# Moving sixteen partition-half swaps from VectorE to GpSimd in a convolution + MLP kernel, with a new instruction order

## The chip, the cores and the metric

The kernel runs on one core of one Trainium2 chip. The metric is the device time of one execution in microseconds (us). Several executions are timed and their median is used; a further execution is recorded by the hardware profiler, and all durations below come from that one.

## The reference

Two layers are applied one after the other to x, 2048 rows by 512 columns in bf16. Each layer is a gated long convolution (A) followed by an MLP (B), each behind a layernorm and with a residual. The convolution's k, v and filters are the same in both layers, so its result y is computed once.

```
kv = (sum over 4 taps of k shifted down by 0..3 rows, times shift_k) * v
y  = irfft(rfft(kv, 4096) * rfft(ssm_k, 4096))[:2048] + kv * ssm_D
twice:
    x = x + layernorm(x) * y
    z = layernorm(layernorm(x))
    x = x + gelu(z @ w1 + b1) @ w2 + b2      # w1 512 x 1376, w2 1376 x 512
```

## The kernel before

**Convolution.** The 2048 rows are split in two halves of 1024, and a Fourier transform of each half is done as matmuls. `stage1` (matmul L630) multiplies the data with a cosine/sine table, `stage2` (matmul L644) with the 4 MB table `tab_s`, which is loaded in four pieces of 1 MB; each of its eight groups needs one half of one piece. A spectrum lies with its real parts in one half of the partitions and its imaginary parts in the other. A complex product therefore needs the filter's spectrum twice: once as it is, and once with the two halves exchanged. The exchange is `swap_v` (L663 on): one 64-partition copy for each half. For the first half of the rows the filter's spectrum is in C3 and the exchanged copy goes to C4, in four pieces, each after two groups of `stage2`; for the second half it goes from C6 to C4. That makes 8 + 8 = 16 copies, all on VectorE (L669). The products follow (`tt`, L534), then the inverse transform: `inverse1` (L682) and `inverse2` (L697). `turn_h` and `turn_k` transpose inputs (L571, L589), and `taps` does the first half's shifts as matmuls (L609) that VectorE multiplies with v (L614). Every matmul group ends with an eviction from PSUM to SBUF by ScalarE (L544) or VectorE (L545).

**MLP.** Eight blocks of 512 rows. For each: statistics (`bn_stats` L894, aggregate L896, a small scaling L901), the power -0.5 on GpSimd (L902), a small VectorE step (L904), normalisation on either engine (L941 ScalarE, L942 VectorE), a transposition by a DMA on SyncE's queue (L999; by TensorE, L1007, for the first block), eleven column groups of the first matmul (L1022) with gelu on ScalarE (L1027), and the second matmul (L1042) with the residual added on VectorE (L1046). The four blocks of the first 1024 rows run while the second half's convolution is spread between their matmuls; then come the four others.

**Order.** Each operation is recorded with an engine (or two to choose from), a duration in ns and what it reads and writes. `schedule` then places them one after the other on each engine by priority, and `sync` adds semaphore waits. The table of numbers handed to `schedule` shifts the priority of single operations. The result is a fixed order for each engine, which runs its list strictly in that order. On GpSimd each instruction that is not the first also waits for the one before it:

```
if e == POOL and o.pos and known[e].get(e, -1) < o.pos - 1:
    need[e] = q[o.pos - 1]
```

The first use of the power L902 makes the compiler put a GpSimd library reload directly ahead of it (MODIFY_POOL_CONFIG in the trace). Before the change, GpSimd has nothing to do but eight small fills, this reload and the 24 powers.

A GpSimd form of the copy is there already, switched off by the flag `PSW` (for the first half alone); it addresses the same bytes as 32-bit words through `W32`:

```
if pool:
    i2, o2 = W32(64 * h, 64, src0 + dg0 * 128 + k0, nd, nk), W32(64 - 64 * h, 64, dst0 + dg0 * 128 + k0, nd, nk)
    P.op(POOL, lambda e, i2=i2, o2=o2: e.tensor_copy(o2, i2), 1500.0, reads=[i], writes=[o])
```

Of the kernel before, what the change touches and what calls it, by code (L numbers as in the profile page):

```python
# [12 lines left out]
PE, ACT, DVE, POOL, SP = "tensor", "scalar", "vector", "gpsimd", "sync"  # L13
# [405 lines left out]
                getattr(block, e)(body)  # L419


WF, SPL, NA1, NDX, KP, KM, SG, PG, PSW, PLN, END, SPS, ST4, IA, SWA = 8, 1, 0, 64, 2, 0, 1, 1, 0, 0, 1, (0, 4), 0, 0, 0
S, D, FF = 2048, 512, 1376
B = 1024
EPS = 1e-5
# [36 lines left out]
AR = 105728  # L462


def bass_interleave_layers__ssm_conv_h3__mixer_channel_mlp__prompt_kernel(
        nc, A_q, A_k, A_v, A_shift_k, A_ssm_k, A_ssm_D, B_x, B_w1, B_b1, B_w2, B_b2, out):
    P = Prog(nc)
# [5 lines left out]
    def A(p0, n, off, *dims):  # L473
        return bass.AP(ar, p0 * AR + off, [[AR, n]] + [list(d) for d in dims])
# [7 lines left out]
    def QB(tile, p0, n, off, *dims):  # L482
        whole = bass.AP(ps, 0, [[4096, 128], [1, 4096]]).bitcast(BF16)
        return bass.AP(whole.tensor, p0 * 8192 + tile.base * 1024 + off, [[8192, n]] + [list(d) for d in dims])
# [6 lines left out]
    def place(n):  # L491
        o = pos[0]
        pos[0] += n
        return o
# [5 lines left out]
    C1, C3, C4, C5, C6 = (place(8192) for _ in range(5))  # L500
# [38 lines left out]
    def evac(dst, src, tile, engs=None, dur=EVD):  # L539
        engs = engs or EV[0]  # L540

        def f(e):
            if e is nc.scalar:
                return e.activation(dst, src(), AF.Copy)  # L544
            return e.tensor_copy(dst, src())  # L545
        return P.op(engs, f, dur, writes=[dst], tile=tile, early=True)
# [109 lines left out]
    def W32(p0, n, off, nd, nk):  # L656

        whole = bass.AP(ar, 0, [[AR, 128], [1, AR]]).bitcast(mybir.dt.int32)
        return bass.AP(whole.tensor, (p0 * AR + off) // 2, [[AR // 2, n], [64, nd], [1, nk // 2]])

    def swap_v(dst0, src0, k0, nk, dg0=0, nd=64, pool=0):
        for h in range(2):
            i = A(64 * h, 64, src0 + dg0 * 128 + k0, [128, nd], [1, nk])  # L663
            o = A(64 - 64 * h, 64, dst0 + dg0 * 128 + k0, [128, nd], [1, nk])
            if pool:
                i2, o2 = W32(64 * h, 64, src0 + dg0 * 128 + k0, nd, nk), W32(64 - 64 * h, 64, dst0 + dg0 * 128 + k0, nd, nk)
                P.op(POOL, lambda e, i2=i2, o2=o2: e.tensor_copy(o2, i2), 1500.0, reads=[i], writes=[o])
            else:
                P.op(DVE, lambda e, i=i, o=o: e.tensor_copy(o, i), 710.0, reads=[i], writes=[o])  # L669

# [70 lines left out]
    for i in range(KP):  # L741
        n = 4096 // KP
# [23 lines left out]
    for i in range(WF):  # L766
        tl = Tile(fill, 0, 8)
        P.op(PE, lambda e, tl=tl, w=w, m=m: e.matmul(Q(tl, 0, 128, 0, [1, 512]), w, m, start=True, stop=True), 216.0,
             reads=[w, m], tile=tl, ni=2, prio=-1e7 - i)
# [10 lines left out]
    for b in range(4):  # L780
        o, i = A(0, 128, R_DG + b * 512, [128, 4], [1, 128]), A(0, 128, R_ID, [0, 4], [1, 128])
        P.op(DVE, lambda e, tl=tl, o=o, i=i, b=b: e.tensor_tensor(o, i, QB(tl, 0, 128, b, [4, 4], [0, 128]), ALU.mult), 620.0,
             reads=[i], writes=[o], tile=tl)
    for i in range(2):
        d0 = A(0, 128, HR[0] + i * 2048, [1024, 2])
        P.op(DVE, lambda e, d0=d0, tl=tl, i=i: e.tensor_tensor(d0, d0, QB(tl, 0, 128, 16 + 2 * i, [1, 2]), ALU.add), 150.0,
             reads=[d0], writes=[d0], tile=tl)
    for j2 in range(2):
# [4 lines left out]
        def f(e, ins=ins, tl=tl):  # L793
            for o, w, m in ins:
                r = e.matmul(Q(tl, 0, 128, o, [1, 128]), w, m, start=True, stop=True)
            return r
# [10 lines left out]
    for g in range(8):  # L807
        stage2(C1, C3, 0, g)
        if g % 2:
            swap_v(C4, C3, 32 * (g // 2), 32, pool=PSW)  # L810
# [33 lines left out]
    for w in range(2 if SG else 4):  # L844
        (shift if SG else shift1)(w)
        n = 4 if SG else 2
        stage1([(KV[1], 0)], C1, 1, range(n * w, n * w + n))
    load_q(1)
    for g in range(4):
        swap_v(C4, C6, 0, 128, 16 * g, 16)  # L850
    for g in range(0, 8192, 4096 if PG else 2048):
        for p in (C6, C4):
            n = 4096 if PG else 2048
            o = A(0, 128, p + g, [1, n])
# [24 lines left out]
    for i in range(2):  # L879
        o = A(96, 1, R_HT + 6144 + i * 512, [1, 512])  # L880
# [55 lines left out]
    def norm(s, mr, o):  # L936
        x = A(0, 128, XS[s], [1, 512])

        def f(e):
            if e is nc.scalar:  # L940
                return e.activation(o, x, AF.Identity, bias=mr[2], scale=mr[1])  # L941
            return e.tensor_scalar(o, x, mr[0], mr[1], ALU.subtract, ALU.mult)  # L942
        if len(mr) == 2:
            P.op(DVE, f, 350.0, reads=[x] + mr, writes=[o])
        else:
            P.op((ACT, DVE), f, {ACT: 715.0, DVE: 340.0}, reads=[x] + mr, writes=[o])
# [3 lines left out]
    def ntmp():  # L950
        nn[0] += 1
        return R_N + (nn[0] % 6) * 512
# [9 lines left out]
    BYPE = (0,)  # L962
    for L, b in [(0, 0), (0, 1), (1, 0), (1, 1), (0, 2), (0, 3), (1, 2), (1, 3)]:
        lo = 2 if b < 2 else 0
        k = blk[0]
# [8 lines left out]
        def lean(i):  # L974
            P.boost = {e: bo[e] + (3e5 if k in SPS and i < 2 else 0.0) for e in bo}
# [17 lines left out]
        for i, s in enumerate(sl):  # L993
            lean(i)
            z = ntmp()
            norm(s, mr[i], A(0, 128, z, [1, 512]))
            if k not in BYPE:
                zs, xt = A(0, 128, z, [1, 512]), A(0, 128, R_XT + (k % 2) * 2048 + i * 128, [512, 4], [1, 128])
                P.op(SP, lambda e, zs=zs, xt=xt: e.dma_start(xt, zs, transpose=True), 1200.0, reads=[zs], writes=[xt],  # L999
                     dma=1250.0, nbytes=1000)  # L1000
                continue
            tl = Tile(ptr, lo)
            src = [A(0, 128, z + 128 * j, [1, 128]) for j in range(4)]

            def f(e, src=src, tl=tl):
                for j in range(4):
                    r = e.transpose(QB(tl, 0, 128, 128 * j, [1, 128]), src[j], IDN)  # L1007
                return r
            P.op(PE, f, 4 * 60.0, reads=src + [IDN], tile=tl, prio=2e5, ni=8)
            evac(A(0, 128, R_XT + (k % 2) * 2048 + i * 128, [512, 4], [1, 128]),  # L1010
                 lambda tl=tl: QB(tl, 0, 128, 0, [128, 4], [1, 128]), tl, dur={ACT: 510.0, DVE: 360.0})
        P.boost = bo
        nt = 256 if k in SPS else 512
        for t0, fc in [(t0, fc) for t0 in range(0, 512, nt) for fc in range(11)]:
# [5 lines left out]
            def f(e, ins=ins, tl=tl, rows=rows, nt=nt):  # L1020
# [8 lines left out]
                reads=[bias], writes=[dst], tile=tl, early=True)  # L1029
        for i, s in enumerate(sl):  # L1030
            last = END and k == 7 and i > 1
            nc2 = 256 if last and i == 3 else 512
            for c0 in range(0, 512, nc2):
# [5 lines left out]
                for l_, h_ in ((0, 4), (4, 8), (8, 11)):  # L1039
                    def f(e, ins=ins, tl=tl, lo=l_, hi=h_, n=nc2):  # L1040
# [6 lines left out]
                     reads=[x], writes=[x], tile=tl)  # L1047
                if L == 1 and last:
                    o = (b // 2) * B * 512 + (s % 8) * 512 + c0
                    outs.append(dma(dr(out, o, [8 * 512, 128], [1, nc2]), x, 256 * nc2, reads=[x], writes=[]))  # L1050
            if L == 1 and i % 2 and not last:
                src = A(0, 128, XS[s - 1], [1, 1024])
                o = (b // 2) * B * 512 + (s % 8 - 1) * 512
                outs.append(dma(dr(out, o, [8 * 512, 128], [1, 1024]), src, 1 << 18, reads=[src], writes=[]))
    P.schedule({
        4: -3072200, 5: -1344100, 6: -833400, 7: -205000, 9: -3255200, 10: -2092700, 11: -3468300, 12: -8512700,
        13: -3019200, 14: -2854800, 16: 973900, 17: -1613800, 18: -3467700, 51: 458300, 53: -280400, 64: -231500,
        85: 1305400, 89: 862600, 91: 1332400, 93: 760800, 97: 753900, 109: 2405500, 111: 2441500, 112: 2165600,
        126: 883500, 128: 759300, 129: -180300, 134: 1496600, 136: 2071800, 138: 1205100, 140: 1205400, 146: 1048500,
        148: 1049100, 150: 418500, 151: 1823100, 152: 1047800, 179: 1627300, 200: 1994100, 220: -232800,  # L1060
        232: -1262000, 236: -1288300, 238: -1567800, 267: 1095500, 336: 774600, 337: 1425000, 338: 807300,
        339: 407300, 350: -346900, 356: 2218500, 357: 751200, 378: -1077000, 379: -1849900, 380: -1179800,
        400: -926000, 422: -422200, 426: -381700, 427: -2063600, 445: 90200, 446: 100700, 447: 73200, 448: 1086400,
        450: -1679000, 453: 1157800, 469: -3094700, 487: -1275200, 500: -637400, 508: -1023900, 556: -539800,
        562: -581600, 564: -853800, 769: 741000, 770: 601100, 772: 696000, 823: -3358400, 831: -5186500,
        837: -4801100, 843: -1187200, 927: 900600, 1013: -288700})
    P.sync()
    P.emit(outs)

# [27 lines left out]
```

## Time and profile before

| | |
|---|---|
| median of 7 executions | 250.72 us (249.99 to 251.68) |
| the profiled execution's own time | 250.25 us |
| its span, first to last instruction | 248.2 us |
| TensorE busy | 234.1 us (94%) |
| VectorE busy | 192.9 us (78%) |
| ScalarE busy | 168.4 us (68%) |
| GpSimd busy | 27.8 us (11%) |
| granted TensorE clock | 1.0 throughout |

The profiled execution takes 2.05 us more than its span. Busy shares are means over stages with different limits: VectorE, at 78% overall, is over 95% busy from about 29 to 150 us. The chain of waits, followed back from the last instruction, shows which engine sets the time in each stage, and the table of stretches shows how much of it the other engines leave idle.

### The profile page before, as it was taken

What the parts mean: (1) busy time and instruction counts of PE and PEld (TensorE: products, weight loads), DVE (VectorE), ACT (ScalarE), POOL (GpSimd) and SP (SyncE); (2) the same over time, 40 slices, a digit from 0 to 9 for tenths busy, and PEclk for the clock granted to TensorE, in tenths of its full rate; (3) what the DMA queues carried; (4) which work ended last, traced back from release to release, by engine and by line L of the source; (5) the groups of instructions that cost most, each with busy time, mean ns of one, the idle gap of its engine ahead of it and who ended that gap; (6) DMA issues with size and microseconds to landing.
All of it is one profiled execution on the core that took longest, in us unless ns stands there. A gap on an engine that the chain in (4) does not pass through costs nothing.

```text
span 248.2 us, 5658 instructions
## 1 busy us (share of the span) xinstructions
PE 234.1 (94%) x2424; PEld 145.3 (59%) x2448; DVE 192.9 (78%) x365; ACT 168.4 (68%) x227; POOL 27.8 (11%) x32
## 2 busy tenths in 40 slices
PE   7999986999899999999799999999999999999995
PEld 4677776896588544455445666447854444444443
DVE  3688999999999999898999997599137966942022
ACT  3596797999999885866786389668823823742810
POOL 0003000000150100402304003021101011020000
PEclk9999999999999999999999999999999999999999
DMA  6999990613001540002692410014400041033002
GB/s 186 384 421 412 398 299 12 235 50 125 3 3 21 176 60 1 0 0 46 127 231 52 100 45 0 3 29 140 90 0 0 0 62 25 0 63 106 3 0 85
DMA packets 22096, 24.78 MB, mean 100 GB/s; under 512 B 15955, under 2 KB 17848, under 8 KB 20664
## 3 DMA queue, kind: packets, MB, share of 16 engines
q1 hardware_dynamic: 21752, 23.34, 30.3%
q10 hardware_dynamic: 320, 1.09, 2.0%
q8 instruction: 19, 0.31, 0.5%
q14 instruction: 5, 0.04, 0.1%
HBM read 16.56 MB, written 2.10 MB: 75 GB/s over the span
## 4 chain that ended last, share of the span: by engine, by line
PE 67%; ACT 12%; DMA 10%; DVE 6%; SPq 2%; issue 1%
PE ps L1022 30%; PE ps L1042 27%; ACT ar L544 11%; DMA ar<-tab_s 7%; PE ps L682 3%; DMA ar<-ar 3%; PE ps L630 2%; PE ps L644 2%; DVE ar L545 2%; PE ps L697 1%; ACT ar L941 1%; SPq L525 1%; DVE ar L669 1%; DVE ar L614 1%; DVE ar L1046 1%
## 5 line engine op out<-in xcount | busy, mean ns | idle before, releaser
L544 ACT ACTIVATE ar<-ps 128x1024 bf16<-128x1024 f32 (+2 forms) x91 | 87.8, 1044 | 26.2 <-PE ps L630 6.5
L1027 ACT ACTIVATE ar<-ps,sm 128x512 bf16<-128x512 f32 (+3 forms) x110 | 64.0, 604 | 35.0 <-PE ps L1022 34.6
L1022 PE MATMUL ps<-ar 128*128 128x512 bf16 (+3 forms) x434 | 78.7, 336 | 2.4 <-DMA ar<-ar 1.8
L1042 PE MATMUL ps<-ar 128*128 128x512 bf16 (+3 forms) x348 | 78.8, 372 | 1.4 <-ACT ar L1027 0.4
L534 DVE TENSOR_TENSOR ar<-ar 128x2048 bf16<-128x2048 bf16 (+2 forms) x76 | 77.0, 1049 | 3.2 <-ACT ar L544 2.8
L1022 PEld LDWEIGHTS ps<-ar 128*128 128x128 bf16 (+1 forms) x440 | 43.3, 100 | 33.9 <-DMA ar<-ar 1.8
L1042 PEld LDWEIGHTS ps<-ar 128*128 128x128 bf16 (+1 forms) x363 | 34.4, 98 | 37.4 <-ACT ar L1027 0.5
L1046 DVE TENSOR_TENSOR ar<-ar,ps 128x512 bf16<-128x512 bf16 (+1 forms) x33 | 21.7, 668 | 33.4 <-PE ps L1042 33.2
L902 POOL TENSOR_TENSOR sm<-sm 128x2 f32<-128x2 f32 (+1 forms) x24 | 26.2, 1093 | 176.9 <-DVE sm L901 170.0
L894 DVE BATCH_NORM_STATS2 sm<-ar 128x6 f32<-128x512 bf16 x64 | 42.7, 684 | 0.3
L630 PE MATMUL ps<-ar 128*64 128x128 bf16 x640 | 22.3, 221 | 1.4 <-ACT ar L544 1.4
L630 PEld LDWEIGHTS ps<-ar 128*64 128x64 bf16 x640 | 18.5, 110 | 7.3 <-ACT ar L544 3.4
L941 ACT ACTIVATE ar<-ar,sm 128x512 bf16<-128x512 bf16 x25 | 19.3, 806 | 5.0 <-DVE sm L904 3.4
L644 PE MATMUL ps<-ar 128*128 128x64 bf16 x512 | 18.8, 193 | 2.9 <-ACT ar L544 1.9
L644 PEld LDWEIGHTS ps<-ar 128*128 128x128 bf16 x512 | 16.7, 98 | 6.9 <-ACT ar L544 3.9
L682 PEld LDWEIGHTS ps<-ar 128*128 128x128 bf16 x256 | 14.8, 98 | 1.9 <-ACT ar L544 0.3
L682 PE MATMUL ps<-ar 128*128 128x128 bf16 x256 | 15.8, 219 | 0.0
L942 DVE TENSOR_SCALAR ar<-ar,sm 128x512 bf16<-128x512 bf16 x39 | 15.5, 421 | 0.3
L669 DVE COPY ar<-ar 64x2048 bf16<-64x2048 bf16 x16 | 10.9, 688 | 0.4
L896 DVE BATCH_NORM_AGGREGATE sm<-sm 128x2 f32<-128x6 f32 x64 | 10.2, 173 | 0.3
L545 DVE CAST ar<-ps 128x1024 bf16<-128x1024 f32 x8 | 9.6, 1219 | 0.6 <-PE ps L644 0.5
L904 DVE SCALAR_TENSOR_TENSOR sm<-sm 128x2 f32<-128x2 f32 (+1 forms) x21 | 3.3, 157 | 7.1 <-POOL sm L902 7.0
(33 smaller groups left out, 69.1 us busy)
## 6 DMA issues: line engine op xcount, KB each, us to landing
ar<-tab_s SPq DMA_DIRECT2D x4, 1024.0 KB, 18.4
ar<-in_A_ssm_k_dram SPq DMA_DIRECT2D x4, 512.0 KB, 6.7
ar<-in_A_q_dram SPq DMA_DIRECT2D x2, 1024.0 KB, 6.9
ar<-in_A_v_dram SPq DMA_DIRECT2D x2, 1024.0 KB, 9.7
out_dram<-ar SPq DMA_DIRECT2D x7, 256.0 KB, 2.3
ar<-in_A_k_dram SPq DMA_DIRECT2D x1, 1408.0 KB, 7.5
ar<-in_B_w_dram SPq DMA_DIRECT2D x1, 1376.0 KB, 22.3
ar<-in_B_w_dram SPq DMA_DIRECT2D x1, 1280.0 KB, 22.9
```

The lines of the kernel that those rows point to most:

```text
L534: return P.op(eng, lambda e: e.tensor_tensor(o, a, b, op), dur, reads=[a, b], writes=[o])
L544: return e.activation(dst, src(), AF.Copy)
L630: r = e.matmul(Q(tl, 64 * ri, 64, i * 128, [1, 128]), w, m, start=j == 0, stop=j == len(terms) - 1)
L644: r = e.matmul(Q(tl, 0, 128, i * nd, [1, nd]), w, m, start=True, stop=True)
L682: r = e.matmul(Q(tl, 0, 128, i * 128, [1, 128]), w, m, start=j == 0, stop=j == len(pp) - 1)
L894: P.op(DVE, lambda e, st=st, x=x: e.bn_stats(st, x), 630.0, reads=[x], writes=[st])
L902: P.op(POOL, lambda e: e.tensor_tensor(r, v, h, ALU.pow), 1200.0, reads=[v, h], writes=[r])
L941: return e.activation(o, x, AF.Identity, bias=mr[2], scale=mr[1])
L1022: r = e.matmul(Q(tl, 0, rows, 0, [1, nt]), w, m, start=dk == 0, stop=dk == 3)
L1027: P.op(ACT, lambda e, dst=dst, tl=tl, rows=rows, bias=bias, nt=nt: e.activation(dst, Q(tl, 0, rows, 0, [1, nt]), AF.Gelu_apprx_tanh, bias= ...
L1042: r = e.matmul(Q(tl, 0, 128, 0, [1, n]), ins[fc][0], ins[fc][1], start=fc == 0, stop=fc == 10)
L1046: P.op(DVE, lambda e, x=x, tl=tl, n=nc2: e.tensor_tensor(x, x, Q(tl, 0, 128, 0, [1, n]), ALU.add), 85.0 + nc2 * 1.055, reads=[x], writes=[ ...
```

## The change

All sixteen copies are given to GpSimd: `PSW` becomes 1, and a new flag `PSH` does the same for the second half. The duration with which the copy is planned is 1050 instead of 1500. `W32` describes the second half's copies (16 x 128 elements that lie together) as one run of 1024 words; the first half's copies (32 elements out of each 128) stay 64 runs of 16 words. The numbers handed to `schedule` are replaced by others, so the order on every engine is another one. The options `BPE`, `TQ` and `SWA` are empty or zero and change nothing.

```
-WF, ..., PSW, PLN, END, SPS, ST4, IA, SWA = 8, 1, 0, 64, 2, 0, 1, 1, 0, 0, 1, (0, 4), 0, 0, 0
+WF, ..., PSW, PLN, END, SPS, ST4, IA, SWA, PSH, BPE, TQ = 8, 1, 0, 64, 2, 0, 1, 1, 1, 0, 1, (0, 4), 0, 0, 0, 1, (), ()
...
-        return bass.AP(whole.tensor, (p0 * AR + off) // 2, [[AR // 2, n], [64, nd], [1, nk // 2]])
+        return bass.AP(whole.tensor, (p0 * AR + off) // 2, [[AR // 2, n], [64, nd], [1, nk // 2]] if nk < 128 else [[AR // 2, n], [1, nd * nk // 2]])
...
-                P.op(POOL, lambda e, i2=i2, o2=o2: e.tensor_copy(o2, i2), 1500.0, reads=[i], writes=[o])
+                P.op(POOL, lambda e, i2=i2, o2=o2: e.tensor_copy(o2, i2), 1050.0, reads=[i], writes=[o])
...
     for g in range(4):
-        swap_v(C4, C6, 0, 128, 16 * g, 16)
+        swap_v(C4, C6, 0, 128, 16 * g, 16, pool=PSH)
...
     P.schedule({
-        4: -3072200, 5: -1344100, 6: -833400, ...
+        4: -2859500, 5: -2332800, 6: -1286000, ...
```

The built program shows what the new order is. On GpSimd (the copies are now L667):

```
before                               after
fill L800                            fill L800
                                     6 copies L667 (first half)
library reload                       library reload
power L902 (128x4) x2                power L902 (128x4) x2
                                     2 copies L667 (first half)
power L902 (128x2) x3                power L902 (128x2) x2
fill L881 x2                         fill, power, fill, power
power L902 (128x2)                   8 copies L667 (second half)
power L902 (128x4), ...              power L902 (128x4), ...
```

On VectorE, the stretch ahead of the first half's products:

```
before                               after
product L614, copies L669 x3         L614 x2, eviction L545 x2 (stage2)
L614, copy, L614, L942               L901 (what the second power reads), L545
eviction L545, L942, copy            L614 x2
L545, copy, L545, copies x2          L942 (waits for the first power)
L942, L545 x2                        L545 (a stage1 group), L942 x3, L545
products L534                        L904 (waits for the second power), L545 x2
                                     products L534 (the second waits for GpSimd's 8th copy)
```

On TensorE the first 96 matmuls of the filter's `stage2` come after two of the four `taps` instead of being strewn between them, and in both orders 160 matmuls of L644 (the filter's last two groups and all eight of the data) stand in one run directly ahead of L571. SyncE's queue loads the first piece of `tab_s` after k and v instead of before; the other three pieces have the same bytes ahead of them as before.

## The prediction

> **What bounds the kernel now.** I began with the chain of waits, because busy shares are means over unlike stages. Its columns are start, length (both us) and what the time is. These are the stretches around the first half's copies and where they end:
>
> ```profile
> 5.93 17.50 DMA ar<-tab_s
> ...
> 25.60 0.57 PE ps L644 x16
> ...
> 29.09 1.23 DVE ar L614
> 30.32 0.03 issue
> 30.35 0.69 DVE ar L669
> ...
> 40.89 1.21 PE ps L571 x16
> 42.10 0.02 issue
> 42.12 16.49 ACT ar L544 x16
> ```
>
> Until 23.4 us a load of tab_s decides, then TensorE to 29.1. From 29.1 to 40.8 every link is on VectorE, five of the swaps (L669) among them; then ScalarE's evictions run without a break. The table of stretches (from:to, length, then busy time and instructions of TensorE, its weight loads, VectorE, ScalarE, GpSimd) says how much each leaves idle:
>
> ```profile
> 29.10:42.10 13.00, 10.69 (x273) 9.47 (x272) 12.73 (x16) 9.60 (x11) 0.00 (x0) 1.00 0.61 201
> 42.10:68.40 26.30, 23.58 (x504) 19.51 (x502) 26.16 (x39) 26.02 (x28) 1.35 (x2) 1.00 0.28 97
> 80.00:95.10 15.10, 14.24 (x184) 7.66 (x184) 14.80 (x26) 12.08 (x16) 1.38 (x1) 1.00 0.40 98
> 95.10:107.40 12.30, 11.82 (x68) 5.73 (x69) 11.40 (x13) 10.20 (x16) 2.98 (x1) 1.00 0.00 0
> 107.40:120.80 13.40, 11.56 (x146) 6.90 (x150) 12.66 (x36) 9.08 (x10) 1.39 (x2) 1.00 0.20 41
> 120.80:165.00 44.20, 43.93 (x295) 24.11 (x300) 39.68 (x77) 31.14 (x42) 7.49 (x6) 1.00 0.31 72
> ```
>
> From 29 to 42 VectorE is full and TensorE lacks 2.3 us; to 68 ScalarE and VectorE are both full and TensorE lacks 2.7; from 80 to 120.8 it lacks 0.86 + 0.48 + 1.84 = 3.2; afterwards almost nothing until the end. So the kernel is TensorE's work plus its gaps: only a gap can shrink, and whatever makes a new gap costs its full length. Last I read GpSimd in order of time, and the listing of the power's line:
>
> ```profile
> 12.83 0.16 POOL L800 MEMSET ar<- 128x64 bf16 x1 [12.00 <-PE ps L768]
> 19.42 1.01 POOL L902 TENSOR_TENSOR sm<-sm 128x4 f32<-128x4 f32 x1 [6.44 <-DVE sm L896]
> 22.63 1.01 POOL L902 TENSOR_TENSOR sm<-sm 128x4 f32<-128x4 f32 x1 [2.20 <-DVE sm L901]
> ...
> 100.74 2.98 POOL L902 TENSOR_TENSOR sm<-sm 128x4 f32<-128x4 f32 x1 [13.40 <-DVE sm L901]
> ```
>
> ```profile
> L902 POOLq MODIFY_POOL_CONFIG  x2: 11/11/11, 12.9 to 12.9; - x2
> ```
>
> The library reload is issued at 12.9, behind the fill at 12.83. The first power starts at 19.42, 0.08 after VectorE's L901 has ended (19.34), the same delay as the second power's. So a reload, whatever it took up to 6.4 us, lay wholly beside other work.
>
> **What the Trainium skill says.** (1) "GPSIMD Engine Reference", "Instruction dispatch": the first call into a freshly loaded library pays about 6 us (5.95 measured) with no visible instruction. The trace neither confirms nor denies it: the gap above holds it exactly. (2) "SBUF — State Buffer", "Who interferes with whom": a VectorE instruction with two SBUF inputs and a reading GpSimd instruction exclude each other; the later waits. The trace agrees: a 128x4 power takes 1.01 alone and 2.98 at 100.74, beside a product of 128x4096 that runs from 100.57 to 102.85. (3) The same "GPSIMD Engine Reference", "Elementwise — side-by-side cycle accounting": a simple body moves an element in 1.03 cycles, at 1.2 GHz 0.88 us for 1024 words; no run here shows such a copy yet.
>
> **The change part by part.**
>
> *Removed.* VectorE loses 16 copies of 688 ns (row L669) = 10.9 us. Of the first eight, three (27.0 to 29.0) lie beside TensorE's links, five on the chain: 5 x 0.69 = 3.4. Next late is ScalarE: its ten evictions from 31.41 take 9.51, to 40.92, and its next starts at 42.12. In the new order it has eleven ahead of that (four of stage1, seven of stage2), 11 x 0.95 = 10.5, to 41.9 from the same start. VectorE's own end could come 3 us earlier, but the next stage, ScalarE's, would gain 0.2 to 1.1; I take 0.7 **if nothing else intervenes**.
>
> *Added on GpSimd.* The fills give a lower price for the copy: 64 elements take 158 ns (L800), 512 take 537 (L881), so 0.85 ns each, and 1024 words 0.97 us; counted as 2048 elements it would be 1.84. I take 1.0 plus 0.1 for the wait on the instruction before, 1.1; ends 0.95 and 1.95.
>
> *The moved reload.* In the new GpSimd order six copies stand ahead of the reload, and the first two powers behind it. On the clock of before: the second piece of tab_s has the same bytes ahead of it and lands at 23.4. The third: landing times of the four have a median of 18.4 with the second's 17.5, so 19.3 after about 6.5 = 25.8. Groups of stage2 take 0.57 on TensorE: the fifth and sixth are done at 26.9, evicted by 28.1. The first copies start when the second group is evicted, 25.1; six at 1.1 end at 31.7. Reload by the page's 6.0: 37.7. First power: 38.7.
>
> Who waits: VectorE's L942, eleventh instruction before the products in its list, needs that power. Its turn is at about 32.3 (taps end at 30.9, the last L614 at 32.1), so it stands until 38.8, and behind it, though ready, L545, the eviction of one stage1 group. All eight groups of the data's stage2 need that group. Thus L942 0.3, L545 1.15 to 40.3; TensorE's run of L644 can go past the filter's two last groups only then. VectorE still has three L942 (1.0), three L545 (3.5) and L904 (0.1): 44.9, against products at 42.06 before, **+2.8**. ScalarE has five of the eight evictions: 41.0 + 5 x 0.95 = 45.8, then its long run, against 42.12, **+3.6**. I take +3.2. With a reload of 5 it is +2.2, with 6.4 +3.6, with nothing -0.7 as above. The two copies behind the powers end near 42, ahead of the product that waits for them. From 42.1 to 68.4 ScalarE has 0.3 us idle, so the delay reaches the MLP's start undiminished, and TensorE is full after it.
>
> *Second half.* The copies write C4, which still holds v and the shift's temporaries, so in both orders they follow the last shift product (83.1 before). VectorE saves 8 x 0.69 = 5.5. But a product of 128x4096 works in place on C6, which the copies read: it must wait for four copies, and while it runs (2.28) GpSimd is locked out. Eight copies at 1.1 and that product make 11.1 us; VectorE has 8.2 of its own work until the next product (three L1046 2.0, five statistics 3.2, aggregates 0.7, the product 2.3), so it waits 2.9 and keeps 2.6 of 5.5. TensorE's gaps from 80 to 120.8 are 3.2 and end in waits on transposes and PSUM that VectorE feeds only in part; I take a gain of 0.8. Ends: 2.2, or a loss of 1.5 at the dearer copy.
>
> *The rest of the order.* One more stage2 group lies ahead of the MLP's start; ScalarE needs 0.95 for it and TensorE 0.47, which it saves later: **+0.4** (0 to +0.6; it is ScalarE's time that sets that start). Loads: only the first piece of tab_s comes later, behind 2.1 MB, about 5 us at 0.41 MB/us, at 19.3, before TensorE asks for it (21.8): nothing; were k or v late instead, up to +1. SyncE's transposes and stores are the same ones, q's second load comes two transposes later and is needed after 95: nothing, -0.3 to +0.5. The flags left empty: nothing.
>
> *Sum.* +3.2 + 0.4 - 0.8 = +2.8 against the profiled execution's 250.25 (span 248.2 and 2.05 around it): 253.05. The median shown is 0.47 above that execution: **253.5**.
>
> **The rivals.** *Reload free* (0.22): the library is already there, or loads beside the copies. Then -0.7 + 0.4 - 0.8 = -1.1, **249.6**. For it: before, the power came at once. Against it: there it had 6.4 us of cover. It decides once the reload takes under about 2.5 us: the stall is then absorbed by ScalarE's lateness. *Relief in full* (0.15): reload free, and the evictions share out so that the whole gap of 2.3 before 42 closes, and half of 3.2: -3.9 + 0.4, **247.2**. For it: VectorE is full from 29 to 150. Against: ScalarE is nearly so. *Slow copies* (0.05): at 1.95 us six end at 36.8, reload and power at 43.8: +8, and the second half loses 1.5; **260**. *The change does nothing* is no case: all sixteen copies change engine.
>
> **How the numbers follow.** A measurement of this kernel can tell about 0.3%, 0.75 us: below 249.97 is faster, above 251.47 slower. The likeliest case, the exposed reload (0.58), gives 253.5 with its own range 251.6 to 255.0; 8% of it falls below 249.97 and 5% between. Reload free splits 65/20/15, the full relief is faster, slow copies are slower. Faster: 0.046 + 0.143 + 0.15 = 0.34; same 0.029 + 0.044 = 0.07; slower 0.59. The range must reach into the free and full cases: 247.7 to 255.2.
>
> **What would show it.** Right: MODIFY_POOL_CONFIG near 31 us, the first power about 6 later, VectorE and TensorE idle from 33 to 39, products from near 45, the MLP's start (first L1022) near 72 instead of 68.4; L667 at 1.0 to 1.1. Wrong: a power within 1 us of the sixth copy, products by 41, first L1022 before 68.5. If L667 takes near 1.9, or the gap comes after 80 us instead, the step on the copies failed and not that on the reload.

## The result, and the profile after

The changed kernel takes 248.44 us (median of 12 runs, 247.97 to 249.25) against 250.87 (31 runs): the ratio is 0.9897, with a 95% interval of 0.9879 to 0.9915, so about 2.4 us, or 1.0%, **faster**. The forecast was 253.5. The profiled execution took 247.97 us with a span of 245.9, which is 2.3 less than before in both; the granted TensorE clock is 1.0 in both.

The step that carried the forecast is read first. This is GpSimd in order of time (start, length, engine, line, operation, and in brackets the idle time before it with what ended it), and the reload's entry in the listing of the power's line:

```profile
13.08 0.16 POOL L800 MEMSET ar<- 128x64 bf16 x1 [12.26 <-PE ps L768]
25.73 6.52 POOL L667 COPY ar<-ar 64x1024 int32<-64x1024 int32 x6 [12.49 <-DVE ar L545]
32.34 2.10 POOL L902 TENSOR_TENSOR sm<-sm 128x4 f32<-128x4 f32 x2
36.42 2.13 POOL L667 COPY ar<-ar 64x1024 int32<-64x1024 int32 x2 [1.99 <-ACT ar L544]
...
83.94 11.54 POOL L667 COPY ar<-ar 64x1024 int32<-64x1024 int32 x8 [4.11 <-DVE ar L534]
97.97 2.98 POOL L902 TENSOR_TENSOR sm<-sm 128x4 f32<-128x4 f32 x1 [2.49 <-DVE sm L901]
```

```profile
L902 POOLq MODIFY_POOL_CONFIG  x2: 8/8/8, 32.2 to 32.2; - x2
```

The six copies end at 32.25, the reload is issued at 32.2, and the power runs at 32.34 with no idle time in front of it. Between reload and power there is 0.1 us, not 6. VectorE in order of time shows what that is worth to those who wait:

```profile
31.10 1.22 DVE L614 TENSOR_TENSOR ar<-ps,ar 128x1024 bf16<-128x1024 f32 x1 [1.19 <-PE ps L609]
33.38 0.41 DVE L942 TENSOR_SCALAR ar<-ar,sm 128x512 bf16<-128x512 bf16 x1 [1.06 <-POOL sm L902]
...
38.66 2.36 DVE L545 CAST ar<-ps 128x1024 bf16<-128x1024 f32 x2 [1.19 <-PE ps L644]
41.12 8.04 DVE L534 TENSOR_TENSOR ar<-ar 128x2048 bf16<-128x2048 bf16 x7
...
95.52 2.29 DVE L534 TENSOR_TENSOR ar<-ar 128x4096 bf16<-128x4096 bf16 x1 [0.97 <-POOL ar L667]
```

L942 stands 1.06 us for the power, as forecast in kind but not in size, and the products begin at 41.12 (42.06 before). VectorE now has idle time ahead of them, and the chain of waits is another one there:

```profile
29.21 1.85 PE ps L609 x14
31.06 0.59 PE ps L630 x16
31.65 0.02 issue
31.67 9.42 ACT ar L544 x10
41.09 0.03 issue
41.12 5.04 DVE ar L534 x5
```

From 31.67 ScalarE carries it with ten evictions, where five links of VectorE's copies stood before. The table of stretches, cut at the same events as before (first products; first L1022; the long runs of L1022 and L1042 in the second half; L1022's resumption), shows where TensorE's idle time went. Columns: from:to, length, then busy time (instructions) of TensorE, its weight loads, VectorE, ScalarE, GpSimd, clock, DMA share, GB/s.

```profile
29.21:41.12 11.91, 10.20 (x258) 8.99 (x258) 8.37 (x11) 10.43 (x11) 7.01 (x7) 1.00 0.68 220
41.12:68.15 27.03, 24.57 (x529) 20.56 (x528) 26.82 (x40) 26.70 (x28) 3.04 (x2) 1.00 0.28 95
80.00:92.24 12.24, 11.87 (x111) 6.29 (x113) 11.26 (x15) 7.54 (x10) 8.00 (x6) 1.00 0.42 118
92.24:106.19 13.95, 13.41 (x116) 7.05 (x117) 12.02 (x17) 11.41 (x17) 6.09 (x4) 1.00 0.01 1
106.19:117.88 11.69, 10.69 (x131) 6.28 (x133) 11.69 (x35) 8.38 (x10) 1.39 (x2) 1.00 0.23 47
```

Length less TensorE's busy time is 1.7, 2.5, 0.4, 0.5 and 1.0. Made over the whole span for both kernels, that ledger reads so (the cut after the second half is at 120.80 before, 117.88 after; TensorE is busy for 234.1 us in both):

| TensorE idle, us | before | after | difference |
|---|---|---|---|
| start to 23.4 | 2.31 | 1.79 | -0.52 |
| 23.4 to the products (42.1; 41.1) | 2.45 | 2.04 | -0.41 |
| to the first L1022 (68.4; 68.15) | 2.72 | 2.46 | -0.26 |
| to 80 | 0.08 | 0.05 | -0.03 |
| 80 to L1022's resumption | 3.18 | 1.91 | -1.27 |
| from there to the end | 3.34 | 3.57 | +0.23 |

The sum is -2.26, the difference of the spans but for rounding. More than half of it lies between 80 us and L1022's resumption, and nearly a quarter ahead of the first copy. Both traces lack some matmul records (2424 and 2425 of 2448 are there), and a missing one counts as up to 0.2 us of idle time. In the row from 80 us seven are missing before and six after (seen against traces of the same orders that have them all), so that this row is sure to about 0.2 us, and the last row's +0.23 can't be told from nothing. Which waits went is named in TensorE's timeline; this is before:

```profile
17.08 1.07 PE L589 MATMUL ps<-ar 128*128 128x128 bf16 x16 [0.47 <-DMA ar<-in_A_k_dram]
...
95.12 8.81 PE L1022 MATMUL ps<-ar 128*128 128x512 bf16 x39 [0.51 <-DMA ar<-ar]
...
120.80 9.44 PE L1022 MATMUL ps<-ar 128*128 128x512 bf16 x43 [1.26 <-DMA ar<-ar]
```

and this is after, the only wait of its kind that is left:

```profile
117.88 2.32 PE L1022 MATMUL ps<-ar 128*128 128x512 bf16 x10 [0.63 <-DMA ar<-ar]
```

The second half lost 0.51 + 0.63 = 1.14 us of waits for a transpose (L999), nearly all of its 1.27; the start lost a wait for k. The chain of waits of the kernel before shows where the first of the two waits for a transpose came from:

```profile
89.12 1.41 ACT ar L941 x2
90.53 0.50 SPq L999
91.08 4.00 DMA ar<-ar
```

ScalarE normalised late (L941), so the block's last transpose was issued at 90.53 and took 4.00 us. In the changed kernel the last transpose of that block is issued at 83.37: of its last three normalisations VectorE does two (L942 at 79.19 and 81.07) and ScalarE one (L941 at 81.11). Ahead of the second wait the chain ran through three of VectorE's adds (L1046) to a transpose that set out at 118.05; the one after the change sets out at 115.11.

### The profile page after: what moved, and what is told of

The parts are those of the page before. It is cut to its first block, busy times and chain, and to the rows that moved or that the text cites. A ratio compares the mean times of both kernels' runs of the same rounds, so it can differ in the third digit from the quotient of the medians.

```text
span 245.9 us, 5661 instructions
## 1 busy us (share of the span) xinstructions
PE 234.1 (95%) x2425; PEld 145.4 (59%) x2448; DVE 184.8 (75%) x353; ACT 164.4 (67%) x223; POOL 49.6 (20%) x48
## 3 DMA queue, kind: packets, MB, share of 16 engines
q10 hardware_dynamic: 320, 1.09, 1.9%
## 4 chain that ended last, share of the span: by engine, by line
PE 63%; DVE 17%; ACT 8%; POOL 8%; issue 2%; DMA 1%; ACTq 1%
PE ps L1042 26%; PE ps L1022 22%; DVE ar L534 12%; ACT ar L544 6%; POOL ar L667 5%; POOL sm L902 3%; PE ps L682 3%; PE ps L609 3%; PE ps L630 2%; DVE sm L894 2%; ACT ar L1027 1%; PE ps L644 1%; PE ps L697 1%; PE ps L762 1%; PE ps L571 1%
## 5 line engine op out<-in xcount | busy, mean ns | idle before, releaser
L544 ACT ACTIVATE ar<-ps 128x1024 bf16<-128x1024 f32 (+2 forms) x89 | 86.0, 1051 | 20.4 <-PE ps L630 8.1
L534 DVE TENSOR_TENSOR ar<-ar 128x2048 bf16<-128x2048 bf16 (+2 forms) x76 | 77.8, 1053 | 5.2 <-ACT ar L544 2.6
L1022 PE MATMUL ps<-ar 128*128 128x512 bf16 (+3 forms) x433 | 80.0, 336 | 1.2 <-DMA ar<-ar 0.6
L1042 PE MATMUL ps<-ar 128*128 128x512 bf16 (+2 forms) x350 | 78.4, 372 | 1.3 <-ACT ar L1027 0.5
L1022 PEld LDWEIGHTS ps<-ar 128*128 128x128 bf16 (+1 forms) x440 | 43.0, 100 | 33.4 <-DMA ar<-ar 0.8
L1042 PEld LDWEIGHTS ps<-ar 128*128 128x128 bf16 (+1 forms) x363 | 34.6, 98 | 38.1 <-ACT ar L1027 0.8
L902 POOL TENSOR_TENSOR sm<-sm 128x2 f32<-128x2 f32 (+1 forms) x24 | 28.7, 1197 | 128.3 <-DVE sm L901 127.5
L1046 DVE TENSOR_TENSOR ar<-ar,ps 128x512 bf16<-128x512 bf16 (+1 forms) x33 | 21.6, 668 | 33.9 <-PE ps L1042 33.8
L941 ACT ACTIVATE ar<-ar,sm 128x512 bf16<-128x512 bf16 x23 | 18.0, 808 | 9.1 <-DVE sm L904 5.6
L667 POOL COPY ar<-ar 64x1024 int32<-64x1024 int32 x16 | 19.4, 1212 | 19.4 <-DVE ar L545 12.5
L644 PE MATMUL ps<-ar 128*128 128x64 bf16 x512 | 18.9, 193 | 3.1 <-ACT ar L544 1.3
L644 PEld LDWEIGHTS ps<-ar 128*128 128x128 bf16 x512 | 16.9, 98 | 6.8 <-ACT ar L544 3.1
L942 DVE TENSOR_SCALAR ar<-ar,sm 128x512 bf16<-128x512 bf16 x41 | 15.7, 409 | 1.6 <-POOL sm L902 1.1
L545 DVE CAST ar<-ps 128x1024 bf16<-128x1024 f32 x9 | 10.8, 1218 | 1.5 <-PE ps L644 1.5
L896 DVE BATCH_NORM_AGGREGATE sm<-sm 128x2 f32<-128x6 f32 x64 | 10.3, 174 | 0.3
```

The source lines that it names most:

```text
L534: return P.op(eng, lambda e: e.tensor_tensor(o, a, b, op), dur, reads=[a, b], writes=[o])
L644: r = e.matmul(Q(tl, 0, 128, i * nd, [1, nd]), w, m, start=True, stop=True)
L667: P.op(POOL, lambda e, i2=i2, o2=o2: e.tensor_copy(o2, i2), 1050.0, reads=[i], writes=[o])
L902: P.op(POOL, lambda e: e.tensor_tensor(r, v, h, ALU.pow), 1200.0, reads=[v, h], writes=[r])
L1022: r = e.matmul(Q(tl, 0, rows, 0, [1, nt]), w, m, start=dk == 0, stop=dk == 3)
L1042: r = e.matmul(Q(tl, 0, 128, 0, [1, n]), ins[fc][0], ins[fc][1], start=fc == 0, stop=fc == 10)
```

## The experiments

Two questions were open: why the reload cost nothing, and what the gain consists of, since the copies' time on VectorE and the new order changed together. In most runs the planned order of every engine is held and only the named copies change engine: `give(x, eng)` takes a copy out of its engine's list and puts it into the other's at the place of its planned start. All times are medians; ratios are against the kernel before, run on the same chip beside them. Copies on VectorE or ScalarE are L666 where L667 is GpSimd's in the changed kernel.

**1. Does a load exist that was merely hidden?** A power nobody needs, and its fill, are put first on GpSimd:

```
+    d0, d1 = M(0, 128, 190, [1, 4]), M(0, 128, 196, [1, 4])
+    P.op(POOL, lambda e: e.memset(d0, 1.0), 100.0, writes=[d0], prio=1e8)
+    P.op(POOL, lambda e: e.tensor_tensor(d1, d0, d0, ALU.pow), 1200.0, reads=[d0], writes=[d1], prio=1e8)
```

> GpSimd is given, as its very first work, a fill of four columns and one power of them that nothing else uses; its library reload so moves from 32.2 us to about 1 us, with no work ahead of it that could hide a load. All orders are otherwise those of the changed kernel. Theory 1 (the reload costs nothing by itself, and the 6 us that stood after it in the kernel before were a wait for statistics): the dummy power starts within 0.3 us of the reload and takes about 1.0 us, and the time is that of the changed kernel, 248.4 within 0.5 us. Theory 2 (a load of about 6 us exists, but it was hidden in the changed kernel, because something before 32.2 us had brought the library in): the dummy power starts 5 to 7 us after the reload; the copies begin only at 25.7 us, so the time is still about 248.4. The gap behind the reload tells the two apart, not the time.

Measured: 248.33 us (ratio 0.9882, 0.9845 to 0.9918). The listing of the new line, then GpSimd's timeline:

```profile
L1057 POOLq MODIFY_POOL_CONFIG  x2: 6/6/6, 0.9 to 1.0; - x2
L1057 POOL TENSOR_TENSOR sm<-sm x1: 1010/1010/1010, 1.1 to 1.1; 128x4 f32<-128x4 f32 x1
```

```profile
1.06 1.01 POOL L1057 TENSOR_TENSOR sm<-sm 128x4 f32<-128x4 f32 x1
```

One microsecond into the program the power follows the reload within 0.1 us and takes its usual 1.01. Nothing in the span could have hidden a load. Theory 1 holds: in this kernel the reload ahead of a power costs nothing. The 6.4 us of idle time behind it in the kernel before need no load to explain them: the power starts 0.08 us after L901 ends (the listing names L896, which comes directly after L901, as what ended the wait). Why it is free stays open: the library may have been there already when the span began, from an earlier execution, or this power may need none. No run here tells these apart.

**2. The copies alone.** The kernel before with its own orders, all sixteen copies on GpSimd:

```
+    for x in P.copies:
+        give(x, POOL)
```

> The instruction order of the kernel before is held on every engine; only the sixteen copies leave VectorE's list and stand in GpSimd's, at the same place in time, behind the two first powers. Theory V (the copies' time on VectorE is what the change removes): VectorE's chain from 29 to 42 us loses 5 x 0.69 us, the products start 1 to 3 us before 42.06, and the time is 248.5 to 249.8. Theory O (the new order is the gain, the copies lay beside ScalarE's equal load): products start within 0.4 us of 42.06 and the time is 250.5 to 251.5. Theory R (rival: the second half's copies on GpSimd are serialised with the in-place products): first half as V, but the gap from 80 to 121 us grows by 1 or more; 250 to 252.

Measured: 250.04 us, ratio 0.9968 (0.9951 to 0.9986). In this profile the products begin at 41.30 and the first L1022 at 67.67, both 0.76 us sooner than before; L1022 resumes at 119.88 (120.80 before):

```profile
41.30 4.63 DVE L534 TENSOR_TENSOR ar<-ar 128x2048 bf16<-128x2048 bf16 x4
...
119.88 6.43 PE L1022 MATMUL ps<-ar 128*128 128x512 bf16 x29 [1.03 <-DMA ar<-ar]
```

The time lies between what theories V and O expected, and the gap that R expected to grow did not: between the first L1022 and its resumption another 0.16 us are gained. So 10.9 us less on VectorE bring 0.8 us; ScalarE and TensorE are next.

**3. The order alone.** The changed kernel's orders, with all sixteen copies on VectorE, then only the first eight, then only the last eight:

```
+    for x in P.copies:         # P.copies[:8], P.copies[8:]
+        give(x, DVE)
```

> The instruction order of the changed kernel is held; only the sixteen copies go back to VectorE, at the place where the plan had them. Theory V: VectorE is behind again, products start at 43 to 45 us instead of 41.1, and the time is 250.5 to 252.5. Theory O: within 0.6 us of the changed kernel, 248.0 to 249.0.

> The changed kernel's order held, the first half's eight copies back on VectorE, the second half's on GpSimd. Theory V says the first half carries most of it (five copies on the chain there): 249.5 to 251.5, products at 43 to 45. If the second half carries it (TensorE's gaps from 80 to 120 shrank by 1.27 of 2.26 us): within 0.5 us of 248.4. Theory O: 248.0 to 249.0.

> The changed kernel's order held, the second half's eight copies back on VectorE. In the trace of the changed kernel the eight copies on GpSimd take 11.5 us (two of them 1.9 and 3.0, beside products) and VectorE then waits 0.97 us for the last one. Theory V: VectorE gets 5.5 us of work back where it is full and the time is 249.0 to 250.0. Theory R: GpSimd's 11.5 us are longer than VectorE's own, so nothing is lost or something gained: 247.6 to 248.6. Theory O: 248.0 to 249.0.

| copies on VectorE, new orders held | us | ratio (95%) |
|---|---|---|
| all sixteen | 255.21 | 1.0176 (1.0150 to 1.0203) |
| first half's eight | 251.14 | 1.0013 (0.9989 to 1.0037) |
| second half's eight | 252.92 | 1.0079 (1.0055 to 1.0103) |

The second is in the range of theory V; the first and the third are slower than any theory had them. A part of that is the clock: in the three profiles it was 0.987, 1.0 and 0.993 and TensorE was busy for 238.1, 236.5 and 237.6 us, so up to about 1.6 us of the first time and 1.1 of the third come from it.

The waits of TensorE (waited for, us in total, times, longest) in the first of these:

```profile
PE ps L1022 <- DVE ar L1046: 4.0, 2, 3.1
PE ps L630 <- DVE ar L614: 2.5, 2, 2.1
```

Neither stands in the changed kernel at more than 0.3. The 2.5 appear alone in the second run of the table and the 4.0 alone in the third: they are the larger part of the 2.7 and 4.5 us that these lose against 248.44. The first is the taps: TensorE waits for L614 behind copies. The second is seen in VectorE's timeline of the third run:

```profile
92.93 2.28 DVE L534 TENSOR_TENSOR ar<-ar 128x4096 bf16<-128x4096 bf16 x1
95.23 2.09 DVE L666 COPY ar<-ar 64x2048 bf16<-64x2048 bf16 x3
97.33 0.69 DVE L1046 TENSOR_TENSOR ar<-ar,ps 128x512 bf16<-128x512 bf16 x1
```

```profile
98.08 4.40 PE L1022 MATMUL ps<-ar 128*128 128x512 bf16 x12 [3.11 <-DVE ar L1046]
```

Three copies between a product and a residual add keep L1046 back, and L1022 is stopped for it. The new order puts work for TensorE directly behind VectorE's adds and taps, which serves only as long as no copies stand between them. It is no gain by itself but a loss of 4.3 us (up to 1.6 of them the clock's), and with the copies gone it is a gain of 1.6 beyond the copies' 0.8.

**4. Is it the move that was planned, or the new numbers?** All copies on GpSimd, planned with the search's numbers of the kernel before, and the reverse:

```
-        4: -2859500, 5: -2332800, 6: -1286000, ...
+        4: -3072200, 5: -1344100, 6: -833400, ...
```

```
-WF, ..., PSW, PLN, END, SPS, ST4, IA, SWA, PSH, BPE, TQ = 8, 1, 0, 64, 2, 0, 1, 1, 1, 0, 1, (0, 4), 0, 0, 0, 1, (), ()
+WF, ..., PSW, PLN, END, SPS, ST4, IA, SWA, PSH, BPE, TQ = 8, 1, 0, 64, 2, 0, 1, 1, 0, 0, 1, (0, 4), 0, 0, 0, 0, (), ()
```

> All sixteen copies on GpSimd, planned by the kernel itself with the order search's numbers of the kernel before: the planner knows of the move, but nothing was searched anew. Theory P (what the move needs is only that the plan knows of it): most of the changed kernel's gain, 248.2 to 249.0 us. Theory S (the new numbers are the second part of the gain): what the move alone brought when the orders of the kernel before were held, 249.6 to 250.4 us.

> The new numbers of the search with all sixteen copies on VectorE, and planned so: unlike the run in which the changed kernel's orders were held and lost 4.5 us against the kernel before, the plan may here put the copies where they do least harm. If the new numbers carried a gain of their own, 249.2 to 250.4 us, faster than before by 0.5 us or more. If they serve only a VectorE that is free of copies, 251 to 255 us; nearer to 251 if the loss of 4.5 us came from where the held order put the copies, nearer to 255 if it came from the order of all the rest.

Measured: 252.05 us, ratio 1.0032 (1.0013 to 1.0050), and 256.11 us, 1.0178 (1.0145 to 1.0211). The first missed both of its theories: planned anew without a new search the move makes the kernel slightly slower. Waits of TensorE in it:

```profile
PE ps L644 <- ACT ar L544: 2.9, 5, 1.0
PE ps L1022 <- DMA ar<-ar: 1.7, 2, 1.5
...
PE ps L1022 <- DVE ar L1046: 1.0, 1, 1.0
```

The transposes' wait of the kernel before is still there, a new one on L1046 has come, and L1022 resumes at 122.17. The second is slower than even the range for numbers that serve only a VectorE free of copies; its granted clock, 0.993 in the profile, has a part in that. The new numbers carry no gain of their own there.

**5. The loads.** The ledger's first row lies ahead of any copy. The first eleven loads of SyncE's queue were exchanged between the two orders (`front` rearranges the head of the queue by the loads' numbers): in the changed kernel, and in the kernel of experiment 2.

```
+    front([16, 8, 7, 6, 15, 5, 10, 17, 4, 9, 14])    # changed kernel, loads as before
...
+    front([8, 16, 6, 7, 15, 5, 17, 4, 14, 9, 10])    # experiment 2, loads as changed
```

> The changed kernel, all orders held but the first eleven loads in SyncE's queue, which go in the order of the kernel before: the first piece of tab_s ahead of the second half of k and of v. Theory L (the 0.5 us that TensorE lacks less before 23.4 us, a wait for k of 0.47 us at 17.08 and one of 0.20 at 18.92 in the kernel before, comes from the loads): the wait for k is back, and the run takes 248.7 to 249.4 us. Theory N (what decides until 23.4 us is when the pieces of tab_s have landed, whichever goes first, so that an earlier matmul gains nothing): 248.4 within 0.4 us.

> The orders of the kernel before held, all sixteen copies on GpSimd, and the first eleven loads in SyncE's queue in the order of the changed kernel. Without the loads this gave 250.04 us. Theory L: 249.3 to 249.8 us, and no wait for k. Theory N: 250.0 within 0.4 us, and what is left to the changed kernel, 1.6 us, is the order on the compute engines.

Measured: 249.28 us, ratio 0.9940 (0.9922 to 0.9957), and 250.31, ratio 0.9979 (0.9956 to 1.0002). In the first, TensorE's waits hold one that the changed kernel has not:

```profile
PE ps L589 <- DMA ar<-in_A_k_dram: 1.8, 1, 1.8
```

Theory L holds there: with the old loads the changed kernel loses 0.8 us. The 1.8 us are too much for that median: the profile is of the slowest of the twelve runs (250.52). They are also more than the 0.47 of the kernel before, which suggests that the new order needs the new loads more than the old order did. In the old order theory L fails and the time is in theory N's range: the new loads bring nothing that can be told from 250.04, although the wait for k is gone in that profile too, and the products begin at 41.14 there against 41.30 without. What takes the gain up was not followed further.

**6. The price of a copy.** The same bytes as 16-bit elements, the changed orders held:

```
-                P.op(POOL, lambda e, i2=i2, o2=o2: e.tensor_copy(o2, i2), ...
+                P.op(POOL, lambda e, i2=i, o2=o: e.tensor_copy(o2, i2), ...
```

> The changed kernel with its orders, GpSimd's sixteen copies moving the same bytes as 2048 elements of 16 bits instead of 1024 of 32. Theory 1 (GpSimd's time follows the number of elements): a copy takes 1.9 to 2.0 us in place of 1.03, the six of the first half end at about 37 us instead of 31.7, the first power moves by about 5 us and the products by 3 to 4, the second half's eight by 7 to 8 us; 255 to 260 us. Theory 2 (it follows the bytes): 1.03 us each and 248.4 within 0.5 us, and the 32-bit words bring nothing.

Measured: 262.46 us, ratio 1.0452 (1.0416 to 1.0487); its granted clock was 0.974, so a part of the time isn't the copies'. The copies' line in this run, and then in the changed kernel (durations least, median, most, in ns):

```profile
L667 POOL COPY ar<-ar x16: 1884/1890/4015, 26.0 to 107.3; 64x2048 bf16<-64x2048 bf16 x16
```

```profile
L667 POOL COPY ar<-ar x16: 1031/1036/2981, 25.7 to 94.4; 64x1024 int32<-64x1024 int32 x16
```

Theory 1 holds, and the loss is even above its range: GpSimd's copy is paid by the element, 1.89 us for 2048 and 1.04 for 1024, so half the elements are 0.85 us less. At the dearer price VectorE stands 8.1 us for the second half's copies (1.0 in the changed kernel). With these orders the move would be a loss without the 32-bit words. The run also shows what a late first power does; it is at 37.7 us here (VectorE's L942: busy, mean ns of one, then its idle time before it and what ended most of that):

```profile
L942 DVE TENSOR_SCALAR ar<-ar,sm 128x512 bf16<-128x512 bf16 x41 | 18.6, 481 | 6.8 <-POOL sm L902 6.2
```

L942 stands 6.2 us for it, and the products begin at 47.84 instead of 41.12. This is the path that the prediction described, with dear copies in place of a dear reload.

**7. Does GpSimd's chain in the second half now set the time?** Eight copies there take 11.54 us, VectorE waits 0.97 for the last, and the chain of waits of the changed kernel runs through all eight. The two long ones in it are:

```profile
85.03 1.93 POOL ar L667
...
90.31 2.99 POOL ar L667
```

Two copies were given to ScalarE, or to VectorE:

```
+    for x in P.copies[12:14]:    # second run: P.copies[14:]
+        give(x, ACT)             # second run: DVE
```

> The changed kernel with its orders, but the fifth and sixth of the second half's eight copies on ScalarE, which idles 1.2 to 2.3 us at a time between 86 and 93 us. It shortens GpSimd's chain of copies by 2 to 3 us and adds about 1.9 us of ScalarE for each. If that chain sets the time (theory R), VectorE's second 4096-wide product starts up to 1.0 us sooner, the wait of 0.97 us ahead of it goes, and the run takes 247.4 to 248.0 us. If it doesn't, because TensorE has no gap between 84 and 100 us (theory T, TensorE's matmuls alone are the bound there), 248.2 to 249 us. Slower by more than 1 us would mean that ScalarE's bias evictions L1027 stand behind the copies and hold TensorE.

> The changed kernel with its orders, but the last two of the second half's eight copies on VectorE, where each takes 0.6 to 0.7 us. If GpSimd's chain of copies sets the time there (theory R), it ends at about 91.5 instead of 95.5 us, VectorE's second product starts after its own copies at about 95.9, and the run takes 247.9 to 248.8 us. If what matters is that nothing stands ahead of VectorE's residual adds L1046 (theory Q, read from the run with all eight on VectorE, which lost 4.5 us), two copies cost little, since the adds of 89.4 and 92.4 us come before them: 248.3 to 249.2 us. A loss in proportion, a quarter of 4.5 us, would give 249.5 us.

Measured: 248.38 us, ratio 0.9891 (0.9864 to 0.9919), and 249.07, ratio 0.9917 (0.9888 to 0.9947). Neither can be told from the changed kernel (0.9879 to 0.9915), and no run here can be said to beat it. The numbering of the copies is that of the program's text; in GpSimd's list those of the first run are the third and fourth, and those of the second run the first two, not the last two as its expectation has it. So only the first run shortens GpSimd's chain: its copies end at 92.46, 3 us sooner, but VectorE now waits 0.98 us for a copy on ScalarE ahead of its first product of 128x4096, and the second begins at 96.53 without waiting. It gains nothing. In the second run VectorE makes its two copies first, and GpSimd's six end at 96.94, no sooner than eight did:

```profile
87.95 8.99 POOL L666 COPY ar<-ar 64x1024 int32<-64x1024 int32 x6 [6.97 <-DVE ar L534]
91.81 3.14 DVE L534 TENSOR_TENSOR ar<-ar 128x4096 bf16<-128x4096 bf16 x1
```

Theory R found no support, but neither run brought the second product forward. That there is little to gain rests on the table of stretches: between 80 and 106 us TensorE lacks only 0.9 us, whatever the chain passes through.

## Why the prediction was wrong, point by point

**The exposed reload: the step that failed.** The sum put +3.2 us there, from 6.0 for the load. It measured 0.1 us at 32.2 (and at 1.0 in experiment 1), so the term is nothing. The path that the stall was to take was read rightly (experiment 6); it had no cause. Of the signs named for being wrong, the power came within 0.1 us of the sixth copy, the first L1022 at 68.15, and the products at 41.12, just past the 41 named. The 6 us came from "GPSIMD Engine Reference", "Instruction dispatch", in the Trainium skill. The same sentence says that they were measured from the reload to the first UNKNOWN instruction, that is, to a freshly loaded kernel's first call; here a TENSOR_TENSOR follows, and the 6 us did not appear. The figure was carried over to another kind of instruction without a measurement of it, and the idle 6.4 us in the kernel before seemed to fit it, though its neighbour, the second power with the same delay of 0.08 after its L901, already explained them in full. The case that a reload is free was seen and got 0.22; with no run or trace that showed a cost, that was too little. Of the two reasons given for it, loading beside the copies is ruled out by experiment 1, where the first copy comes 25 us after the power; that the library was already there is not.

**The arithmetic around it was sound.** Copies from 25.1 to 31.7 were forecast, they ran from 25.73 to 32.25; a copy and its wait at 1.1, measured 6.52/6 = 1.09 (the copy alone 1.04, above the 0.88 estimated from the cycles of "GPSIMD Engine Reference", "Elementwise — side-by-side cycle accounting"); L942's turn at 32.3, it stood from 32.3 to 33.38, with a power of 1.0 in place of a load and a power.

**First half without the reload: right in sum, in part by luck.** The forecast was -0.7 to the products, limited by ScalarE, and +0.4 for one more group ahead of the MLP: together -0.3 at the first L1022. Measured -0.94 and -0.28: the two terms missed by a quarter of a microsecond each, in opposite directions. The copies alone gave -0.76 with the old order, and a part of the -0.94 may be the earlier start that the loads brought. The limit named, ScalarE's evictions, is the one in the chain: ten from 31.67 on, where eleven were forecast.

**Second half: undersized.** The forecast was -0.8, with GpSimd's eight copies and one product at 11.1 us (measured 11.54) and a wait of VectorE's of 2.9 (measured 0.97). The lockout is that of "SBUF — State Buffer", "Who interferes with whom", and the trace agrees: two of the eight copies took 1.93 and 2.99 us beside products, six 1.04 to 1.05. The gap from 80 us on shrank by 1.27. The copies' part of that is small: in the old order, L1022 resumed only 0.16 us sooner, once the 0.76 from the first half are taken off. The rest is the order, in which the waits for two transposes go; the first of them goes because normalisations come sooner, a cause that the forecast did not name.

**The rest of the order: the missing term.** The loads were put at nothing, with "v or k late" as the only other end; they gave 0.5 in the ledger, and in experiment 5 0.8 under the new order and nothing under the old, so they have no price of their own. It was seen that the first piece of tab_s goes behind k and v, but only what would then be late was asked, not what would come sooner. Of the rival without a reload, 249.6, the measurement is 1.2 us below, and loads and second half (-0.52 and -0.47 beyond the term) are 1.0 of these. "Relief in full", 247.2, came nearer in time, for reasons it did not have: the gap ahead of 42 us did not close (2.45 to 2.04).

Left open: the half of the last 1.6 us that experiment 5 doesn't cover was located by waits (transposes, 1.14), not by a run that changes only when the transposes set out.

## What to carry to other kernels

A price from a page holds for what it was measured on, until a run shows it for one's own case; where the trace's idle time is explained by a wait that needs no such price, the wait is the better reading. Work moved off an engine that is busy 95% of a stretch brings only what the next engine leaves (here 0.8 of 10.9 us); its larger value may be that an order becomes possible in which the bound engine is fed directly, and then neither part can be priced alone: the order alone lost 4.3 us, a part of it the clock's, the move alone gained 0.8, both gained 2.4. When an order changes, go through the queues for what comes earlier as well as for what comes late.

## What the runs showed of the hardware that was not expected

- A library reload ahead of a power on GpSimd took no time that the trace shows: power 0.1 us after it, at 32.2 us as at 1.0 us.
- GpSimd's copy of 64 partitions costs 1.04 us for 1024 elements of 32 bits and 1.89 for the same bytes as 2048 of 16 bits; VectorE's copy of the latter took 0.69 and ScalarE's 1.91 (the first run of experiment 7).
- Beside VectorE's product of 128x4096 a copy on GpSimd took up to 2.99 us instead of 1.04, and in the second run of experiment 7 the product itself 3.14 instead of 2.29, so either side can be the one that waits.
